# Five of eight row tiles of w_mod[gb] kept in PSUM, transposed, from the modulation stage to the end of the FFN

## The chip, the cores and the metric

The kernel runs on one core of one Trainium2 chip. The metric is device time in microseconds (us), from the start of the program to its end, the median of several executions. PE is TensorE (PEld its weight loads), DVE is VectorE, ACT is ScalarE, POOL is GpSimd and SP is SyncE. "L206" in a profile line is line 206 of the kernel that was profiled; the changed kernel and the experiments have other line numbers for the same helpers (L206 becomes L213, L171 becomes L172).

## The reference, cut to what matters

The program computes one decoder block and its gradients with respect to all its inputs. The block is modulated: six vectors of 1024 come from `silu(c) @ w_mod`, where `w_mod` is 1024 x 6144, six sections of 1024 columns.

```python
mod = (_silu(c) @ w_mod).reshape(c.shape[0], 6, 1, -1)
sa, ca, ga, sb, cb, gb = (mod[:, 0], mod[:, 1], mod[:, 2], mod[:, 3], mod[:, 4], mod[:, 5])
h = _layernorm(x) * (1 + ca) + sa
x = x + ga * _A_ref(h, k_cache, v_cache, wq, wo)      # attention, 4096 keys of 65536
h = _layernorm(x) * (1 + cb) + sb
x = x + gb * _B_ref(h, w_gate, w_up, w_down)          # FFN of 3584
```

The gradient of `c` needs `w_mod @ dmod`: each of the 1024 rows of `w_mod` times the gradient of the six vectors. The part for `gb` (section 5) is `w_mod[:, 5*1024:] @ (grad_out * ffn)`, so it can only be formed after the FFN. The gradients of the caches are zero outside the last 4096 keys, so the kernel must write some 126 MB of zeros.

## The kernel before

`w_mod` is loaded once at the start, in eight row tiles of 128 x 6144 (1.5 MB each). Each tile gives its share of `mod` and is then transposed by PE, section by section, into PSUM; DVE and ACT carry sections 0 to 4 from there to SBUF, where they wait, transposed, for the gradient of `c`. For section 5 the kernel keeps no room in SBUF. It is loaded again at the end (256 KB for each row tile), and DVE forms its product-sum with the gradient.

```python
psum = tc.tile_pool(name="psum", bufs=3, space=PSUM)      # [128, 512] f32, also tm_w
pacc = tc.tile_pool(name="pacc", bufs=2, space=PSUM)      # small accumulators
phold = tc.tile_pool(name="phold", bufs=1, space=PSUM)    # the FFN's sum
ptp = tc.tile_pool(name="ptp", bufs=2, space=PSUM)        # transposes
...
def mod_transpose(j):
    tps = {}
    for sct in (1, 0, 2, 3, 4):
        tp = tps[sct] = new_tp("tp_w") if sct < 2 else new_tm("tm_w")
        for nb in range(KD):
            c0 = sct * D + nb * P
            nc.tensor.transpose(tp[:, nb * P:(nb + 1) * P], wm_t[j][:, c0:c0 + P], ident_bf[:, :])
    ...                                   # evacuations: two on DVE, three on ACT
for j in range(KD):                       # eight row tiles
    for k in range(KM):                   # 48 columns of mod
        mm = nc.tensor.matmul(mod_ps[:, k:k + 1], lhsT=wm_t[j][:, k * P:(k + 1) * P], ...)
    if j < KD - 1:
        mod_transpose(j)
    zero(Z_MOD[j], mm)                    # zero writes, paced by this matmul
    ...
# last stages
def sec_load(j):
    nc.sync.dma_start(out=sec_t[j][:, 3 * D:4 * D], in_=wm_view[:, j, 5 * D:6 * D])
def sec(j, nz):
    w5 = sec_t[j][:, 3 * D:4 * D]
    ttr(w5, w5, dmod_b4[:, 3 * D:4 * D], dcs[:, j:j + 1])      # product-sum on DVE
    outer_dve(sec_t[j], cs_col[:, j:j + 1], dmod_b4)           # gradient of w_mod
    nc.gpsimd.dma_start(out=dwm_view[:, j, 2048:6144], in_=sec_t[j])
    zero(nz)
sec_load(0)
sec_load(1)
for q4 in range(8):                       # dWo: four product-sums, four outer products each
    ...
    nc.gpsimd.dma_start(out=wo_rows(out_5, q4), in_=wo_t[q4])
    zero(Z_DWO[q4])
    ...
# then dS, dq; sec_load(2) to sec_load(7); sec(0), sec(1); dWq with kv gradients and sec(2) to sec(7)
```

POOL issues most writes, among them the zeros: `zero(n)` puts n writes of 1 MB each behind whatever POOL has issued, so that the DMA queues have work while the engines compute. The counts in lists such as `Z_DWO` pace them.

Of the kernel before, what the change touches and what calls it, by code (L numbers as in the profile page):

```python
# [34 lines left out]
SCALE = DH ** -0.5  # L35
KIB = 512


# [23 lines left out]
def kernel(  # L62
# [29 lines left out]
    pool = ctx.enter_context(tc.tile_pool(name="sb", bufs=1))  # L92
    psum = ctx.enter_context(tc.tile_pool(name="psum", bufs=3, space=bass.MemoryType.PSUM))
    pacc = ctx.enter_context(tc.tile_pool(name="pacc", bufs=2, space=bass.MemoryType.PSUM))
    phold = ctx.enter_context(tc.tile_pool(name="phold", bufs=1, space=bass.MemoryType.PSUM))
    ptp = ctx.enter_context(tc.tile_pool(name="ptp", bufs=2, space=bass.MemoryType.PSUM))

# [76 lines left out]


    def new_ps(name="ps"):
        return psum.tile([P, 512], FP32, name=name, tag="mm")

# [3 lines left out]
    def new_tp(name="tp"):  # L182
        return ptp.tile([P, 1024], BF16, name=name, tag="tp")

    def new_tm(name="tm"):
        return psum.tile([P, 1024], BF16, name=name, tag="mm")

# [6 lines left out]
    def addv(out, a, b):  # L194
        return tt(out, a, b, ALU.add)

    def cp(out, a):
        return nc.vector.tensor_copy(out=out, in_=a)  # L198
# [43 lines left out]
    def col_to_row_out(col_f, dram_out_row, name):  # L242
        rp = ptp.tile([8, P], FP32, name="rp_" + name, tag="tp")
        nc.tensor.transpose(rp[:, :], col_f, ident_f[:, :])
        rowb = pool.tile([8, P], BF16, name=name + "_orow", tag=name + "_orow")
        cp(rowb, rp[:, :])
        nc.sync.dma_start(out=dram_out_row.rearrange("o (j p) -> (o j) p", p=P), in_=rowb)
# [73 lines left out]

    tp0 = ptp.tile([P, 24], BF16, name="tp_rows", tag="tp")
    nc.tensor.transpose(tp0[:, :], rows24[:, :], ident_bf[0:24, 0:24])
    vecs = vt([P, 24], "vecs")
    cp(vecs, tp0[:, :])
    x0_col, go_col, c_col = vecs[:, 0:8], vecs[:, 8:16], vecs[:, 16:24]
# [16 lines left out]
    def mod_transpose(j):  # L343
        tps = {}
        for sct in (1, 0, 2, 3, 4):
            tp = tps[sct] = new_tp("tp_w") if sct < 2 else new_tm("tm_w")
            for nb in range(KD):
                c0 = sct * D + nb * P
                nc.tensor.transpose(tp[:, nb * P:(nb + 1) * P], wm_t[j][:, c0:c0 + P], ident_bf[:, :])  # L349
        cols = slice(j * P, (j + 1) * P)  # L350
        v = {k: tp.rearrange("p (n m) -> p n m", n=KD) for k, tp in tps.items()}
        mulv(w01_tmp, v[1], ln1.rearrange("p (n o) -> p n o", o=1).broadcast_to([P, KD, P]))
        addv(w01_T[:, :, cols], w01_tmp, v[0])
        nc.scalar.copy(out=w2_T[:, :, cols], in_=v[2])
        nc.scalar.copy(out=w34_T[:, :, 0, cols], in_=v[3])
        nc.scalar.copy(out=w34_T[:, :, 1, cols], in_=v[4])

    mod_ps = new_acc("mod_ps")
    for j in range(KD):
# [235 lines left out]

    ffn_ps = phold.tile([P, KD], FP32, name="ffn_ps")
    dh2acc = vt([P, NB * KD], "dh2acc")
# [8 lines left out]
    def front(n):  # L606
        ug, wd = ug_slot[n % 3], wd_slot[n % 2]
        r = small[n % 2]
        gu = gu_t[n] = new_acc("gu_ps")
        for col, k in ((2, 0), (0, 1)):  # L610
            for jj in range(2):
                for j in range(KD):
                    nc.tensor.matmul(gu[:, col + jj:col + jj + 1], lhsT=ug[:, k, j, jj::2],  # L613
                                     rhs=h2_bf[:, j:j + 1], start=(j == 0), stop=(j == KD - 1))
        nc.scalar.activation(out=r["sg"], in_=gu[:, 0:2], func=ACT.Sigmoid)  # L615
        nc.scalar.activation(out=r["om"], in_=gu[:, 0:2], func=ACT.Sigmoid, scale=-1.0)
# [50 lines left out]
    ffn = vt([P, KD], "ffn")  # L667
    cp(ffn, ffn_ps[:, :])
    dh2 = vt([P, KD], "dh2")
# [10 lines left out]
    dmod_bf = vt([P, KM], "dmod_bf", BF16)  # L680
    mulv(dmod_bf[:, 40:48], go_col, ffn)
    cp(dmod_bf[:, 24:32], dh2)
# [29 lines left out]
    def sec(j, nz):  # L712
        w5 = sec_t[j][:, 3 * D:4 * D]
        ttr(w5, w5, dmod_b4[:, 3 * D:4 * D], dcs[:, j:j + 1])
        outer_dve(sec_t[j], cs_col[:, j:j + 1], dmod_b4)
        nc.gpsimd.dma_start(out=dwm_view[:, j, 2048:6144], in_=sec_t[j])
        zero(nz)

    sec_load(0)
    sec_load(1)  # L720

# [24 lines left out]
    for q4 in range(8):  # L746
# [10 lines left out]
        if q4 < 2:  # L757
            bcast(dmod_bf[:, 16 + 16 * q4:32 + 16 * q4], 16, dmod_b4[:, 2048 * q4:2048 * (q4 + 1)], "A")
        elif q4 < 6:
            rebuild_P(q4 - 2)  # L760
        elif q4 == 6:
            build_e()
# [24 lines left out]
    for ch in range(8):  # L787
        ps = new_ps("dp_ps")
        for g in range(G):
# [4 lines left out]
                                       in1=P_bf[:, ch * 512:(ch + 1) * 512], op0=ALU.subtract, op1=ALU.mult)  # L794
    sec_load(2)
    sec_load(3)
    dsT = transpose_rows(dS, "dsT", "AAAA")
    DO_hd = make_hd(do_col2, "DO_hd")
    sec(0, Z_SEC[0])
    dq_ps, mm = av_like(k_nat, dsT, "dq")  # L800
    for k in range(4, 8):
        sec_load(k)
# [109 lines left out]
```

## Time and profile before

| | before |
|---|---|
| median of 4 executions | 624.12 us (623.96 to 624.36) |
| span of the profiled execution | 622.2 us |
| moved by DMA | 256.42 MB, mean 412 GB/s |
| busiest engine | DVE, 326.3 us (52%) |

From the groups by shape (line, engine, operation, output <- inputs, shapes, count | busy us, mean ns | idle time before and what ended it): the product of a transposed PSUM tile with a vector, and the product-sums of section 5.

```profile
L189 DVE TENSOR_TENSOR arena<-tp_w,ln_ln 128x1024 f32<-128x1024 bf16 x8 | 9.8, 1224 | 16.2 <-PE tp_w L349 16.2
L206 DVE CUSTOM_DVE_ANT_0 arena<-arena 128x1024 bf16<-128x1024 bf16 x8 | 9.8, 1219 | 29.9 <-DMA arena<-in_w_mod_dram 29.9
```

The reader is to see the durations, 1.22 us each, and that all the idle time before the product-sums, 29.9 us, is one wait for the reloads.

From the timeline of PE in the modulation stage (start, duration, count): the 48 `mod` matmuls of two consecutive row tiles.

```profile
25.67 1.35 PE L361 MATMUL mod_ps<-cs_bf,arena 128*128 128x1 bf16 x48 [0.57 <-DMA arena<-in_w_mod_dram]
29.25 1.35 PE L361 MATMUL mod_ps<-cs_bf,arena 128*128 128x1 bf16 x48
```

One row tile takes 3.6 us here. What PE waits for is data (0.57 us before the first of the two); no wait for a bank shows.

### The profile page before, as it was taken

The numbers are of one execution on the slowest core, as the hardware profiler recorded it, in microseconds if no ns is written. First come the engines' busy times: TensorE is split into PE (matmuls) and PEld (weight loads), VectorE is DVE, ScalarE is ACT, GpSimd is POOL, SyncE is SP. The second block draws the span as 40 slices with busy tenths as digits, with TensorE's granted clock in tenths as the row PEclk, the third lists the DMA queues.
The fourth block names the chain that finished last, engine by engine and source line by source line (L and its number), as shares of the span: only waits on it lengthen the run. The fifth ranks groups of instructions, "written<-read, shape, count | busy, mean of one in ns | idle before, by whom it ended". The sixth has DMA issues, their size and how long they took to land.

```text
span 622.2 us, 8426 instructions
## 1 busy us (share of the span) xinstructions
PE 186.5 (30%) x3324; PEld 163.6 (26%) x3324; DVE 326.3 (52%) x728; ACT 212.5 (34%) x333; POOL 148.2 (24%) x232
## 2 busy tenths in 40 slices
PE   3977266623022111111011111133039100455100
PEld 3967155623012111111011111122017100344100
DVE  3442037302969385544556554469997306994400
ACT  2652147200026143322133333239847101455300
POOL 2001021113222433223343322342211111222420
PEclk9976578755555555555555555555557555555555
DMA  9999999999999999999999999999999999999997
GB/s 351 422 421 421 421 418 420 423 425 423 423 403 408 408 410 410 411 411 408 411 411 409 411 412 409 413 419 414 427 426 421 423 424 419 428 426 425 423 424 273
DMA packets 42647, 256.42 MB, mean 412 GB/s; under 512 B 5149, under 2 KB 5149, under 8 KB 18080
## 3 DMA queue, kind: packets, MB, share of 16 engines
q0 software_dynamic: 31568, 192.95, 80.6%
q1 hardware_dynamic: 10992, 62.93, 29.9%
q8 instruction: 26, 0.43, 0.3%
q14 instruction: 13, 0.11, 0.0%
q10 hardware_dynamic: 48, 0.01, 0.0%
HBM read 70.26 MB, written 185.60 MB: 411 GB/s over the span
## 4 chain that ended last, share of the span: by engine, by line
DMA 59%; DVE 12%; issue 11%; PE 8%; POOL 4%; ACT 3%; ACTq 0%; POOLq 0%; SPq 0%; DVEq 0%
DMA out_dram<-arena 28%; DMA out_dram<-zeros 11%; DVE arena L206 7%; DMA arena<-in_w_mod_dram 6%; DMA arena<-in_B_w_gate_dram 5%; DMA arena<-in_A_k_cache_dram 4%; DMA arena<-in_B_w_down_dram 3%; PE tp_kv L440 2%; ACT arena L443 1%; PE tm_w L349 1%; DVE arena L202 1%; POOL out_dram L657 1%; POOL arena L540 1%; POOL out_dram L171 1%; PE tp_w L349 1%
## 5 line engine op out<-in xcount | busy, mean ns | idle before, releaser
L171 POOL DMA_DIRECT2D out_dram<-zeros x114 | 63.0, 556 | 179.8 <-DMA out_dram<-zeros 55.5
L237 ACT ACTIVATE arena<-dug_b,h 128x512 bf16<-128x512 bf16 x112 | 71.4, 713 | 13.3 <-DVE dh2acc L206 13.3
L206 DVE CUSTOM_DVE_ANT_0 arena<-arena,dug_b 128x512 bf16<-128x512 bf16 x112 | 69.6, 686 | 0.1
L206 DVE CUSTOM_DVE_ANT_0 arena<-arena 128x1024 bf16<-128x1024 bf16 (+1 forms) x16 | 45.1, 2819 | 32.3 <-DMA arena<-in_w_mod_dram 29.9
L613 PE MATMUL gu_ps<-h_bf,arena 128*128 128x1 bf16 x448 | 16.2, 166 | 144.8 <-issue 92.1
L613 PEld LDWEIGHTS <-arena 128*128 128x128 bf16 x448 | 14.2, 105 | 146.9 <-issue 92.6
L206 DVE CUSTOM_DVE_ANT_0 junk<-arena,b1k 128x1024 fp8e4<-128x1024 bf16 x28 | 34.3, 1224 | 29.3 <-DMA arena<-in_B_w_down_dram 28.8
L823 PEld LDWEIGHTS <-arena 8*128 8x128 bf16 x256 | 24.9, 127 | 72.9 <-issue 69.5
L615 ACT ACTIVATE sg<-gu_ps 128x2 f32<-128x2 f32 x14 | 2.4, 168 | 111.0 <-PE gu_ps L613 111.0
L206 DVE CUSTOM_DVE_ANT_0 arena<-arena,b1k 128x1024 bf16<-128x1024 bf16 x32 | 37.2, 1220 | 0.0
L540 POOL DMA_DIRECT2D arena<-in_B_w_up_dram x14 | 12.8, 918 | 88.8 <-DMA out_dram<-arena 48.3
L827 ACT CAST arena<-ps_kv 128x512 bf16<-128x512 f32 x32 | 16.1, 692 | 44.2 <-DMA out_dram<-arena 44.2
L237 ACT ACTIVATE arena<-b1k,o_sh 128x1024 bf16<-128x1024 bf16 x24 | 27.2, 1151 | 11.0 <-DVE do_sh L206 11.0
L189 DVE TENSOR_TENSOR dug<-dhh,sg 128x2 f32<-128x2 f32 x14 | 2.3, 161 | 53.5 <-ACT sg L615 52.9
L440 PE MATMUL tp_kv<-ident_bf,arena 128*128 128x128 bf16 x256 | 22.4, 255 | 21.5 <-DMA arena<-in_A_k_cache_dram 13.8
L823 PE MATMUL ps_kv<-DO_hd,arena 8*128 8x128 bf16 x128 | 15.3, 279 | 45.0 <-ACT arena L827 44.2
L198 DVE COPY arena<-tp_kv 128x1024 bf16<-128x1024 bf16 x19 | 13.1, 691 | 29.2 <-PE tp_kv L440 29.2
L637 PE MATMUL bc_ps<-ident_bf,dug_bf 128*128 128x128 bf16 x56 | 14.5, 475 | 44.9 <-DVE hh L189 44.9
L440 PEld LDWEIGHTS <-arena 128*128 128x128 bf16 x256 | 19.6, 116 | 24.3 <-DMA arena<-in_A_k_cache_dram 14.7
L349 PEld LDWEIGHTS <-arena 128*128 128x128 bf16 x320 | 24.9, 121 | 0.0
L443 ACT COPY arena<-tp_kv 128x1024 bf16<-128x1024 bf16 x13 | 13.1, 1010 | 32.5 <-PE tp_kv L440 32.5
L829 ACT ACTIVATE arena<-ps_kv 128x512 bf16<-128x512 f32 x32 | 16.1, 625 | 21.6 <-DMA out_dram<-arena 21.6
(228 smaller groups left out, 503.8 us busy)
## 6 DMA issues: line engine op xcount, KB each, us to landing
out_dram<-zeros POOLq DMA_DIRECT2D x114, 1024.0 KB, 16.3
out_dram<-arena POOLq DMA_DIRECT2D x32, 1024.0 KB, 17.7
out_dram<-arena POOLq DMA_DIRECT2D x36, 512.0 KB, 13.3
arena<-in_A_wq_dram SPq DMA_DIRECT2D x16, 1024.0 KB, 15.8
arena<-in_w_mod_dram SPq DMA_DIRECT2D x8, 1536.0 KB, 20.3
arena<-in_A_wo_dram SPq DMA_DIRECT2D x8, 1024.0 KB, 39.7
arena<-in_B_w_down_dram SPq DMA_DIRECT2D x14, 512.0 KB, 11.5
arena<-in_B_w_up_dram POOLq DMA_DIRECT2D x14, 512.0 KB, 11.7
```

The lines of the kernel that those rows point to most:

```text
L171: ins = nc.gpsimd.dma_start(out=region.bitcast(FP32), in_=zeros[:, :])
L206: return nc.vector.tensor_tensor_reduce(out=out, in0=w, in1=b, scale=1.0, scalar=0.0, op0=ALU.mult, op1=ALU.add, accum_out=acc)
L237: return nc.scalar.activation(out=out, in_=b, func=ACT.Copy, scale=col)
L349: nc.tensor.transpose(tp[:, nb * P:(nb + 1) * P], wm_t[j][:, c0:c0 + P], ident_bf[:, :])
L440: nc.tensor.transpose(tp[:, t8 * P:(t8 + 1) * P], src[:, g, t_ * DH:(t_ + 1) * DH], ident_bf[:, :])
L443: last = nc.scalar.copy(out=o, in_=tp[:, :])
L540: nc.gpsimd.dma_start(out=ug_slot[n % 3][:, k, :, :], in_=view[:, :, n * FB:(n + 1) * FB])
L613: nc.tensor.matmul(gu[:, col + jj:col + jj + 1], lhsT=ug[:, k, j, jj::2], rhs=h2_bf[:, j:j + 1], start=(j == 0), stop=(j == KD - 1))
L637: nc.tensor.matmul(ps4[:, k // 2, :, k % 2], lhsT=r["dug_bf"][:, k:k + 1].broadcast_to([P, P]), rhs=ident_bf[:, :], start=(k == 0), stop=( ...
L823: nc.tensor.matmul(ps[:, t4 * DH:(t4 + 1) * DH], lhsT=rows[32 * g:32 * g + HG, t_ * P:(t_ + 1) * P], rhs=hd[32 * g:32 * g + HG, :], start= ...
L827: nc.scalar.copy(out=o, in_=ps[:, :])
L829: nc.scalar.activation(out=o, in_=ps[:, :], func=ACT.Copy, scale=float(scale))
```

## The change

The intent is to save reloads without room in SBUF. PSUM has eight banks; a transposed row tile of section 5 (128 x 1024 bf16) fills one. Five tiles stay parked there from the modulation stage to the end of the FFN. Everything else shares three banks: two that rotate, for transposes and for [128, 512] results alike, and one accumulator. At the end of the FFN the parked tile is multiplied with the gradient vector (which lies along the partitions, since the tile is transposed), summed over its eight blocks, and summed over the partitions by a matmul with ones. After that the five banks join the rotation. Three reloads remain. The diff, cut to its core:

```diff
+PARK = 5
-    psum = ... name="psum", bufs=3
-    pacc = ... name="pacc", bufs=2
-    phold = ... name="phold", bufs=1
-    ptp = ... name="ptp", bufs=2
+    psum = ... name="psum", bufs=7 - PARK
+    pacc = ... name="pacc", bufs=1
+    ppark = ... name="ppark", bufs=PARK
     ...
     def mod_transpose(j):
-        tps = {}
         for sct in (1, 0, 2, 3, 4):
-            tp = tps[sct] = new_tp("tp_w") if sct < 2 else new_tm("tm_w")
+            tp = new_tp("tp_w")
             ...                                # transposes, then at once the evacuation
+        if j < PARK:
+            park[j] = ppark.tile([P, D], BF16, name="park", tag="pk")
+            for nb in range(KD):
+                c0 = 5 * D + nb * P
+                nc.tensor.transpose(park[j][:, nb * P:(nb + 1) * P], wm_t[j][:, c0:c0 + P], ident_bf[:, :])
     ...
-    ffn_ps = phold.tile([P, KD], FP32, name="ffn_ps")
+    ffn_ps = new_acc("ffn_ps")[:, 0:KD]
-        gu = gu_t[n] = new_acc("gu_ps")
+        gu = gu_t[n] = new_ps("gu_ps")
     ...
-        ttr(w5, w5, dmod_b4[:, 3 * D:4 * D], dcs[:, j:j + 1])
+        if j >= PARK:
+            ttr(w5, w5, dmod_b4[:, 3 * D:4 * D], dcs[:, j:j + 1])
-    sec_load(0)
-    sec_load(1)
+    def park_products():
+        prod = dS.bitcast(FP32)
+        pm = prod[:, 0:D].rearrange("p (n m) -> p n m", n=KD)
+        col = dgb.rearrange("p (n o) -> p n o", o=1).broadcast_to([P, KD, P])
+        for j in range(PARK):
+            mulv(pm, park[j].rearrange("p (n m) -> p n m", n=KD), col)
+            nc.vector.reduce_sum(out=prod[:, D + j * P:D + (j + 1) * P], in_=pm.rearrange("p n m -> p m n"), axis=AX.X)
+        ps = new_acc("gb_ps")
+        for j in range(PARK):
+            nc.tensor.matmul(ps[:, j:j + 1], lhsT=prod[:, D + j * P:D + (j + 1) * P], rhs=ones_f[:, 0:1], ...)
+        cp(dcs[:, 0:PARK], ps[:, 0:PARK])
     ...
         elif q4 < 6:
+            if q4 == 2:
+                park_products()
+                rot.append((ppark, "pk"))
             rebuild_P(q4 - 2)
     ...
-    sec_load(2)
-    sec_load(3)
+    for k in range(PARK, 4):
+        sec_load(k)
     ...
-    for k in range(4, 8):
+    for k in range(max(PARK, 4), 8):
         sec_load(k)
```

More of the change, by code (lines that the diff above doesn't have):

```diff
@@ L92 @@
     pool = ctx.enter_context(tc.tile_pool(name="sb", bufs=1))
-    psum = ctx.enter_context(tc.tile_pool(name="psum", bufs=3, space=bass.MemoryType.PSUM))
-    pacc = ctx.enter_context(tc.tile_pool(name="pacc", bufs=2, space=bass.MemoryType.PSUM))
-    phold = ctx.enter_context(tc.tile_pool(name="phold", bufs=1, space=bass.MemoryType.PSUM))
-    ptp = ctx.enter_context(tc.tile_pool(name="ptp", bufs=2, space=bass.MemoryType.PSUM))
+    psum = ctx.enter_context(tc.tile_pool(name="psum", bufs=7 - PARK, space=bass.MemoryType.PSUM))
+    pacc = ctx.enter_context(tc.tile_pool(name="pacc", bufs=1, space=bass.MemoryType.PSUM))
+    ppark = ctx.enter_context(tc.tile_pool(name="ppark", bufs=PARK, space=bass.MemoryType.PSUM))
     arena = pool.tile([P, 192 * KIB], BF16, name="arena")
@@ L173, in zero, with next_pool @@
                 dep(first or ins, after)
+    rot = [(psum, "mm")]
+    nrot = [0]
+    def next_pool():
+        nrot[0] += 1
+        return rot[nrot[0] % len(rot)]
     def new_ps(name="ps"):
-        return psum.tile([P, 512], FP32, name=name, tag="mm")
+        p, tag = next_pool()
+        return p.tile([P, 512], FP32, name=name, tag=tag)
     def new_acc(name="acc"):
@@ L182, in new_tp @@
     def new_tp(name="tp"):
-        return ptp.tile([P, 1024], BF16, name=name, tag="tp")
-    def new_tm(name="tm"):
-        return psum.tile([P, 1024], BF16, name=name, tag="mm")
+        p, tag = next_pool()
+        return p.tile([P, 1024], BF16, name=name, tag=tag)
     def tt(out, a, b, op):
@@ L242, in col_to_row_out @@
     def col_to_row_out(col_f, dram_out_row, name):
-        rp = ptp.tile([8, P], FP32, name="rp_" + name, tag="tp")
-        nc.tensor.transpose(rp[:, :], col_f, ident_f[:, :])
+        rp = new_ps("rp_" + name)[0:8, 0:P]
+        nc.tensor.transpose(rp, col_f, ident_f[:, :])
         rowb = pool.tile([8, P], BF16, name=name + "_orow", tag=name + "_orow")
-        cp(rowb, rp[:, :])
+        cp(rowb, rp)
         nc.sync.dma_start(out=dram_out_row.rearrange("o (j p) -> (o j) p", p=P), in_=rowb)
@@ L320 @@
     nc.gpsimd.dma_start(out=rest[NS:8, 0:nlen * 128], in_=zeros[0:8 - NS, 0:nlen * 128])
-    tp0 = ptp.tile([P, 24], BF16, name="tp_rows", tag="tp")
-    nc.tensor.transpose(tp0[:, :], rows24[:, :], ident_bf[0:24, 0:24])
+    tp0 = new_tp("tp_rows")[:, 0:24]
+    nc.tensor.transpose(tp0, rows24[:, :], ident_bf[0:24, 0:24])
     vecs = vt([P, 24], "vecs")
-    cp(vecs, tp0[:, :])
+    cp(vecs, tp0)
     x0_col, go_col, c_col = vecs[:, 0:8], vecs[:, 8:16], vecs[:, 16:24]
@@ L343, in mod_transpose @@
     def mod_transpose(j):
-        tps = {}
+        cols = slice(j * P, (j + 1) * P)
         for sct in (1, 0, 2, 3, 4):
-            tp = tps[sct] = new_tp("tp_w") if sct < 2 else new_tm("tm_w")
+            tp = new_tp("tp_w")
             for nb in range(KD):
@@ L349, in mod_transpose @@
                 nc.tensor.transpose(tp[:, nb * P:(nb + 1) * P], wm_t[j][:, c0:c0 + P], ident_bf[:, :])
-        cols = slice(j * P, (j + 1) * P)
-        v = {k: tp.rearrange("p (n m) -> p n m", n=KD) for k, tp in tps.items()}
-        mulv(w01_tmp, v[1], ln1.rearrange("p (n o) -> p n o", o=1).broadcast_to([P, KD, P]))
-        addv(w01_T[:, :, cols], w01_tmp, v[0])
-        nc.scalar.copy(out=w2_T[:, :, cols], in_=v[2])
-        nc.scalar.copy(out=w34_T[:, :, 0, cols], in_=v[3])
-        nc.scalar.copy(out=w34_T[:, :, 1, cols], in_=v[4])
+            v = tp.rearrange("p (n m) -> p n m", n=KD)
+            if sct == 1:
+                mulv(w01_tmp, v, ln1.rearrange("p (n o) -> p n o", o=1).broadcast_to([P, KD, P]))
+            elif sct == 0:
+                addv(w01_T[:, :, cols], w01_tmp, v)
+            elif sct == 2:
+                nc.scalar.copy(out=w2_T[:, :, cols], in_=v)
+            else:
+                nc.scalar.copy(out=w34_T[:, :, sct - 3, cols], in_=v)
+        if j < PARK:
[3 more added lines that the diff above has]
+                nc.tensor.transpose(park[j][:, nb * P:(nb + 1) * P], wm_t[j][:, c0:c0 + P], ident_bf[:, :])
+    park = {}
     mod_ps = new_acc("mod_ps")
@@ L667 @@
     ffn = vt([P, KD], "ffn")
-    cp(ffn, ffn_ps[:, :])
+    cp(ffn, ffn_ps)
     dh2 = vt([P, KD], "dh2")
@@ L680 @@
     dmod_bf = vt([P, KM], "dmod_bf", BF16)
-    mulv(dmod_bf[:, 40:48], go_col, ffn)
+    dgb = vt([P, KD], "dgb")
+    mulv(dgb, go_col, ffn)
+    cp(dmod_bf[:, 40:48], dgb)
     cp(dmod_bf[:, 24:32], dh2)
@@ L717, in sec @@
         zero(nz)
-    sec_load(0)
-    sec_load(1)
+    def park_products():
[7 more added lines that the diff above has]
+        for j in range(PARK):
+            nc.tensor.matmul(ps[:, j:j + 1], lhsT=prod[:, D + j * P:D + (j + 1) * P], rhs=ones_f[:, 0:1],
+                             start=True, stop=True)
+        cp(dcs[:, 0:PARK], ps[:, 0:PARK])
     def rebuild_P(tb):
```

## The prediction

> **What bounds the kernel now.** I read the page's slices first. The first line below is the busy share of the 16 DMA engines in 40 equal slices of the span (9 means 90% or more), the second what they moved in each, the third the total.
>
> ```profile
> DMA  9999999999999999999999999999999999999997
> GB/s 351 422 421 421 421 418 420 423 425 423 423 403 408 408 410 410 411 411 408 411 411 409 411 412 409 413 419 414 427 426 421 423 424 419 428 426 425 423 424 273
> DMA packets 42647, 256.42 MB, mean 412 GB/s; under 512 B 5149, under 2 KB 5149, under 8 KB 18080
> ```
>
> The reader is to see that no slice but the first and the last falls off: outside the FFN (403 to 419) the queues move 418 to 428 GB/s whatever the engines do. 256.42 MB at 412 GB/s is 622 us, the whole span. So the kernel is bound by the bytes it moves, and a change is worth the bytes that it removes, unless it lets the queues run dry.
>
> Second, the windows view (columns: length, busy time and count of PE, weight loads, DVE, ACT, POOL; granted clock, DMA share, GB/s), for the stretches that the change touches late in the kernel:
>
> ```profile
> 430.00:440.00 10.00, 2.83 (x104) 2.46 (x96) 9.93 (x17) 8.62 (x9) 2.79 (x5) 0.50 1.14 428
> 440.00:450.00 10.00, 0.91 (x36) 0.64 (x24) 9.93 (x19) 8.68 (x8) 2.13 (x4) 0.50 1.12 426
> 450.00:460.00 10.00, 0.00 (x0) 0.10 (x1) 9.87 (x22) 7.35 (x7) 1.60 (x3) 0.50 1.18 424
> 490.00:518.00 28.00, 0.00 (x0) 0.00 (x0) 0.00 (x0) 0.00 (x0) 3.22 (x6) 0.50 1.08 423
> 518.00:567.00 49.00, 19.35 (x156) 15.68 (x156) 48.56 (x39) 20.04 (x40) 11.09 (x17) 0.50 1.05 425
> ```
>
> From 430 to 460 us DVE is full, from 490 to 518 us all compute engines do nothing, and the DMA rate is the same in both. The listing of waits says what the 28 us are, and what holds POOL, which issues most of the writes:
>
> ```profile
> POOL out_dram L171 <- DMA out_dram<-zeros: 55.5, 35, 3.2
> DVE arena L206 <- DMA arena<-in_w_mod_dram: 29.9, 1, 29.9
> ```
>
> POOL waits for earlier zero writes to land before it may issue more: the write queue is full. DVE waits once, 29.9 us, for reloaded w_mod rows, the very transfers that the change partly removes. Those 29.9 us look like the prize; they are not, because the DMA works through them.
>
> Third, how deep the queue is. A 1024 KB zero write takes 16.3 us from issue to landing in the median (the page's DMA issues), but 1.05 MB at 424 GB/s is only 2.5 us, so some 14 us of other work stands ahead of it. Summing bytes issued minus bytes of packets ended over the trace gives the same: 5 to 8 MB outstanding (12 to 19 us) from 405 to 520 us, 6.8 to 9 MB from 25 to 60 us, and minima of 2.5 MB (6 us) near 140 us and 2.0 MB (5 us) near 575 us.
>
> **What the Trainium skill says.** "DMA: Bandwidth & Descriptors", section "Where 436 GB/s comes from", puts the ceiling of the 16 ports at 435 GB/s; the trace agrees, with 418 to 428 held for most of the span: there is no faster rate to win, only fewer bytes. "VectorE: DVE Perf Modes", sections "The perf-mode tier table" and "Why PSUM operands drop a tier", says that a product of two tensors with one in PSUM, and any reduction, runs at one element a cycle; the trace agrees for the product: 128x1024 from a transposed PSUM tile takes 1224 ns. "PSUM — Partial Sum Buffer", "Specifications (TRN2)": 8 banks of 2 KiB a partition; a transposed 128x1024 bf16 tile fills one, so five parked tiles leave three. "TensorE: Matmul & The Clock Gate", Part 1, says that idleness halves the PE clock; here eight transposes take about 0.93 us before 21 us and 0.52 us at 22 to 33 us, so a PE that waits more may also run slower.
>
> **The change part by part.**
>
> (a) Removed: five of the eight w_mod reloads at the end, 256.0 KB each: 5 x 262,144 B = 1.31 MB. At the 424 GB/s of that stretch: 3.1 us of DMA time, on the path, since the DMA is the path. Also five product-sums 128x1024 of 1.22 us (the x8 group: 1219 ns), 6.1 us of DVE beside it.
>
> (b) Added on DVE, in the dWo stage after the third of eight blocks: five products from PSUM at 1.22 us (same shape and types as the 128x1024 f32<-bf16 rows of the modulation stage) and five strided f32 reductions of 1024. No row has this reduction; my estimate from one element a cycle is 1.2 us, and from the 128x112 strided row (0.35 us, 1.9 ns an element above a small one's 0.15) 2.0 us. Sum 12 to 16 us, plus about 1 us for five small f32 matmuls and a copy: 13 to 17 us of DVE in a stage where DVE is full. Is it on the path? POOL issues the dWo blocks late because its queue is full. In the timeline (start, duration, line; in brackets its idle time):
>
> ```profile
> 447.89 0.53 POOL L755 DMA_DIRECT2D out_dram<-arena  x1 [2.25 <-ACT arena L237]
> 450.32 0.53 POOL L755 DMA_DIRECT2D out_dram<-arena  x1 [1.90 <-DVE do_sh L206]
> 452.75 0.53 POOL L755 DMA_DIRECT2D out_dram<-arena  x1 [1.90 <-ACT arena L237]
> ```
>
> These are blocks 2, 3 and 4, which DVE finished at about 434, 439 and 444 us: POOL lags DVE by 9 to 14 us. Delayed by 15 us, block 3 is ready at 454 and block 4 at 459, so they go out 4 and 6 us late, against 17 us outstanding at 450 us (7.3 MB). The queue thins, but doesn't empty. The chain after it (dS, dq, first dWq) starts about 15 us later; then the 29.9 us wait is gone for rows 2 to 4, which need no reload, so DVE makes up what it lost. I expect DVE's work through the last dWq to end before the 567 us of before. The ends of the last stage are set by the two kv-gradient buffers coming free, as before.
>
> (c) Moved to fewer banks: the modulation stage rotates two banks where it had five, so each of the five section transposes waits for an evacuation (DVE 1.22 us, ACT 1.02 us). Per row tile, worked out by hand: tile pair 1.0, product 1.2, sum 1.2, then copies of 1.0 chained with the transposes, then eight parked transposes 0.5 and the 48 columns of mod 1.3: about 5.9 us with the fast clock, 7.5 with the slow, against 3.6 and 5.6 in the trace. PE falls 6 to 8 us behind, of which later tiles' waits for data take back little: q starts at about 60 us, not 52.5. Parked transposes: 40 x 65 to 117 ns = 2.6 to 4.7 us of PE, in that sum. Loads of w_mod 5 to 7 and of K are issued later by the same, but 6.8 to 9 MB are outstanding then (16 to 21 us). By my sum at least 4 MB stay ahead. So hidden.
>
> (d) FFN, scores and kv gradients: gate/up results and broadcasts now share two banks, but each is read before its bank is next wanted; the FFN total takes the one accumulator bank, which nothing else wants meanwhile; after the parked products the five banks join the rotation. I charge nothing.
>
> Sum: 624.0 - 3.1 = 620.9 us.
>
> **The rivals.** 1, the path is DVE's: the chain that ended last runs through DVE product-sums from 418 to 459 us and through the w_mod reload at 502 us. If the chain were the bound, +15 us of DVE and -30 us of wait would give about 610 us, or 637 if the wait is not recovered. Against it: the DMA moves 423 to 428 GB/s through both stretches. 2, the queue runs dry: either at 60 to 68 us, if PE stays at the slow clock in the modulation stage (K loads 12 or more us late), or near 450 to 490 us, if the reductions cost more than 2 us each. Each dry microsecond adds one; I could believe 2 to 5 us, giving 621 to 626. 3, a transfer that is hidden anyway: if the 1.31 MB only filled gaps, the time would stay 624; but no gap shows in the slices where they move. 4, fewer holes at the end: 2.0 MB outstanding at 575 us goes with 410 GB/s, so an earlier DVE could win a few tenths.
>
> **Range and chances.** The byte term is firm (2.9 to 3.3 us). Rival 2 is the main spread, upward; rival 4 is small, downward. Predicted 620.9 us, 8 in 10 between 619.6 and 624.0. Faster by over 2% needs 611.5 us, four times the bytes removed: 0.01. Slower by over 2% needs 636.5 us, 15 us of empty queue: 0.02. Within 2%: 0.97.
>
> **What would show it.** Moved bytes 255.1 MB instead of 256.4 at the same mean rate (411 to 413 GB/s). The 29.9 us wait gone or below 10 us, without the time following it. Products at 1.2 us, reductions 1.2 to 2 us; DVE 13 to 17 us busier around 434 to 450 us with 415 to 428 GB/s kept. q's matmuls starting at 58 to 64 us, still 418 or more GB/s before and after. The prediction is wrong if a slice in the middle falls below 400 GB/s, or if the span falls by much more than bytes over rate.

## The result, and the profile after

| | before | after |
|---|---|---|
| median | 624.12 us (4 executions, 623.96 to 624.36) | 620.90 us (4 executions, 620.81 to 621.34) |
| ratio | 1 | 0.9949, 95% interval 0.9932 to 0.9967 |
| span of the profiled execution | 622.2 us | 619.0 us |
| moved by DMA | 256.42 MB | 255.11 MB |
| DVE busy | 326.3 us | 335.4 us |

A ratio is the mean time of one kernel's executions over that of the other's of the same rounds, so it is not quite the ratio of the medians quoted. The result lies within 2%: 3.2 us, 0.5%.

The page of the changed kernel, as the prediction showed it for the one before: busy share of the DMA engines in 40 slices, what they moved, the total.

```profile
DMA  9999999999999999999999999999999999999997
GB/s 350 424 424 420 397 420 423 425 420 425 425 405 402 410 412 409 412 405 412 411 412 409 411 409 411 412 415 421 426 425 425 422 422 423 425 427 425 427 421 287
DMA packets 41927, 255.11 MB, mean 412 GB/s; under 512 B 5069, under 2 KB 5069, under 8 KB 17360
```

The reader is to see the same mean rate, 412 GB/s, 1.31 MB fewer, and one new flaw: the fifth slice (62 to 77 us) fell to 397 GB/s.

The windows view for that stretch, kernel before and then kernel after (columns as in the prediction: length, busy time and count of PE, weight loads, DVE, ACT, POOL; granted clock, DMA share, GB/s):

```profile
62.00:77.00 15.00, 4.11 (x56) 3.24 (x56) 0.98 (x3) 1.95 (x2) 1.64 (x4) 0.50 1.13 421
```

```profile
62.00:77.00 15.00, 10.65 (x290) 10.40 (x290) 1.66 (x5) 2.94 (x3) 3.16 (x6) 0.50 1.05 398
430.00:450.00 20.00, 2.85 (x12) 2.40 (x10) 19.21 (x17) 3.85 (x5) 4.79 (x9) 0.50 1.13 427
490.00:518.00 28.00, 10.65 (x92) 9.12 (x91) 23.71 (x13) 10.76 (x22) 6.31 (x10) 0.50 1.08 422
518.00:567.00 49.00, 19.72 (x160) 16.33 (x160) 32.92 (x29) 20.10 (x40) 10.79 (x18) 0.50 1.05 426
```

From 490 to 518 us, where all compute engines had idled, DVE is now busy for 23.7 of 28 us, and the DMA moves 422 GB/s instead of 423. What the engines do there does not matter to the time.

What the added work costs on DVE, from the groups by shape:

```profile
L744 DVE TENSOR_REDUCE arena<-arena 128x128 f32<-128x1024 f32 x5 | 9.4, 1871 | 0.2
L196 DVE TENSOR_TENSOR arena<-park,dgb 128x1024 f32<-128x1024 bf16 x5 | 6.1, 1223 | 0.1
```

Products of 1.22 us and reductions of 1.87 us: with starts 3.2 us apart, 16.5 us from 433.8 to 450.3 us, the copy included. The timeline of POOL shows what that delays (dWo blocks 2, 3 and 4, now L784):

```profile
447.35 0.53 POOL L784 DMA_DIRECT2D out_dram<-arena  x1 [2.23 <-DMA out_dram<-zeros]
456.05 0.53 POOL L784 DMA_DIRECT2D out_dram<-arena  x1 [8.17 <-DVE arena L209]
461.14 0.53 POOL L784 DMA_DIRECT2D out_dram<-arena  x1 [4.56 <-ACT arena L759]
```

Block 3 goes out at 456.0 instead of 450.3 us and block 4 at 461.1 instead of 452.8 us, and POOL now waits for DVE there, 8.2 us. The queue (the bytes issued and not yet moved) held 7.0 MB at 450 us and at least 4.1 MB from there to 500 us, so the rate did not move.

The chain that ended last, by line, is a trap worth seeing:

```profile
DMA out_dram<-arena 29%; DMA out_dram<-zeros 21%; DMA arena<-in_B_w_gate_dram 5%; DVE arena L213 4%; DVE arena L196 4%; DMA arena<-in_B_w_down_dram 3%; PE tp_w L356 3%; PE mod_ps L377 2%; DVE arena L744 2%; POOL out_dram L673 1%; POOL arena L556 1%; DMA rows<-in_c_dram 1%; PE q_ps L416 1%; POOL out_dram L172 1%; DVE arena L209 1%
```

It runs through the reductions (L744) and the products (part of L196) that were just added. Yet the kernel got faster, and nothing of them shows in the time: it fell by what the bytes are worth.

In the modulation stage, two consecutive row tiles on PE:

```profile
25.07 1.34 PE L377 MATMUL mod_ps<-cs_bf,arena 128*128 128x1 bf16 x48
31.87 1.34 PE L377 MATMUL mod_ps<-cs_bf,arena 128*128 128x1 bf16 x48
```

6.8 us a row tile instead of 3.6. The PE clock, by its records, changes between half and full every 3.4 us here. The q matmuls began at 64.9 us (before: 52.6 us). K and V loads wait for this stage's tiles to come free, and zero writes wait for the q matmuls, so the queue ran down to 0.8 MB at 64 us. Bytes moved up to a given time, summed from the packets' ends, put a number on it:

```
time us   before MB   after MB   difference, in us of 420 GB/s
   60       23.95       24.03      +0.2
   90       36.53       36.19      -0.8
  410      168.48      168.15      -0.8
  490      202.09      201.93      -0.4
  610      252.97      252.80      -0.4
```

So this execution lost 0.8 us in the modulation stage and kept the loss through the FFN. It had 1.31 MB less to move (3.1 us), regained 0.4 us between 410 and 490 us, and the last packets and the end of the program gained the rest: the span is 3.1 us shorter.

### The profile page after: what moved, and what is told of

It reads as the page before. It is cut to its first block, busy times and chain, and to the rows that moved or that the text cites. A ratio compares the mean times of both kernels' runs of the same rounds, so it can differ in the third digit from the quotient of the medians.

```text
span 619.0 us, 8520 instructions
## 1 busy us (share of the span) xinstructions
PE 196.1 (32%) x3374; PEld 172.6 (28%) x3374; DVE 335.4 (54%) x730; ACT 213.8 (35%) x333; POOL 148.8 (24%) x232
## 2 busy tenths in 40 slices
DMA packets 41927, 255.11 MB, mean 412 GB/s; under 512 B 5069, under 2 KB 5069, under 8 KB 17360
## 3 DMA queue, kind: packets, MB, share of 16 engines
HBM read 68.95 MB, written 185.60 MB: 411 GB/s over the span
## 4 chain that ended last, share of the span: by engine, by line
DMA 59%; DVE 13%; issue 11%; PE 9%; POOL 4%; ACT 1%; ACTq 0%; POOLq 0%; DVEq 0%; SPq 0%
DMA out_dram<-arena 29%; DMA out_dram<-zeros 21%; DMA arena<-in_B_w_gate_dram 5%; DVE arena L213 4%; DVE arena L196 4%; DMA arena<-in_B_w_down_dram 3%; PE tp_w L356 3%; PE mod_ps L377 2%; DVE arena L744 2%; POOL out_dram L673 1%; POOL arena L556 1%; DMA rows<-in_c_dram 1%; PE q_ps L416 1%; POOL out_dram L172 1%; DVE arena L209 1%
## 5 line engine op out<-in xcount | busy, mean ns | idle before, releaser
L172 POOL DMA_DIRECT2D out_dram<-zeros x114 | 63.0, 554 | 189.6 <-DMA out_dram<-zeros 61.5
L629 PEld LDWEIGHTS <-arena 128*128 128x128 bf16 x448 | 14.3, 105 | 142.8 <-DMA arena<-in_B_w_up_dram 95.8
L213 DVE CUSTOM_DVE_ANT_0 arena<-arena 128x4096 bf16<-128x4096 bf16 (+1 forms) x11 | 39.0, 3546 | 4.8 <-ACT arena L302 4.8
L356 PE MATMUL tp_w<-ident_bf,arena 128*128 128x128 bf16 x320 | 33.7, 285 | 8.5 <-DVE arena L196 8.5
L356 PEld LDWEIGHTS <-arena 128*128 128x128 bf16 x320 | 29.3, 132 | 10.9 <-issue 10.9
L196 DVE TENSOR_TENSOR dug<-dhh,sg 128x2 f32<-128x2 f32 x14 | 2.2, 160 | 51.9 <-ACT sg L631 51.5
L196 DVE TENSOR_TENSOR arena<-tp_w,ln_ln 128x1024 f32<-128x1024 bf16 x8 | 9.8, 1223 | 26.8 <-PE tp_w L356 26.8
L861 ACT ACTIVATE arena<-ps_kv 128x512 bf16<-128x512 f32 x32 | 16.1, 627 | 20.8 <-DMA out_dram<-arena 20.8
L855 PE MATMUL ps_kv<-Q_hd,arena 8*128 8x128 bf16 x128 | 15.8, 302 | 21.1 <-ACT arena L861 21.1
L556 POOL DMA_DIRECT2D arena<-in_B_w_gate_dram x14 | 12.7, 910 | 39.5 <-issue 20.7
```

The lines of the kernel that those rows point to most:

```text
L172: ins = nc.gpsimd.dma_start(out=region.bitcast(FP32), in_=zeros[:, :])
L196: return nc.vector.tensor_tensor(out=out, in0=a, in1=b, op=op)
L213: return nc.vector.tensor_tensor_reduce(out=out, in0=w, in1=b, scale=1.0, scalar=0.0, op0=ALU.mult, op1=ALU.add, accum_out=acc)
L556: nc.gpsimd.dma_start(out=ug_slot[n % 3][:, k, :, :], in_=view[:, :, n * FB:(n + 1) * FB])
L629: nc.tensor.matmul(gu[:, col + jj:col + jj + 1], lhsT=ug[:, k, j, jj::2], rhs=h2_bf[:, j:j + 1], start=(j == 0), stop=(j == KD - 1))
L855: nc.tensor.matmul(ps[:, t4 * DH:(t4 + 1) * DH], lhsT=rows[32 * g:32 * g + HG, t_ * P:(t_ + 1) * P], rhs=hd[32 * g:32 * g + HG, :], start= ...
```

## The experiments

The theory: the time is the bytes over a rate of some 420 GB/s, plus whatever time the queues run dry; waits and engine time count only if they make them dry. The main rival: the gain comes from the wait of 29.9 us that vanished, or from what VectorE does (the chain runs through it). A second rival: the two-bank rotation takes something back.

"Queue" below is the bytes of all DMAs issued up to a moment less the bytes of the packets ended by then. The experiments of one call ran on the same chip, against executions of the kernel before on it (medians 624.00 to 624.09 us).

**Control.** The experiments avoid one instruction form of the kernel, the product-sum with an fp8 output: its element-wise output goes to a scratch tile that nobody reads. All of them store it as uint8.

```diff
-    junk = vt([P, D], "junk", FP8)
+    junk = vt([P, D], "junk", mybir.dt.uint8)
```

> Control: the changed kernel with one scratch tile of the FFN (the element-wise output of the product-sums, which nobody reads) stored as uint8 instead of fp8; every later experiment carries this edit. Both theories: 620.9 us, within 0.3 us of the changed kernel, product-sums of 128x1024 still 1.22 us. If it is off by more, the others are compared with this control.

Measured: 620.85 us (5 executions, 620.71 to 621.41), ratio 0.9950, interval 0.9937 to 0.9962. The edit is neutral, and the control stands for the changed kernel.

**The bytes put back, without the wait.** The five reloads return. They are issued when they were before, two at 418 us and three from 503 us (before: 417 and 502 us). Three go into the room of a row tile that is filled later, two into their own, long before it is written; no engine reads them.

```diff
+    sec_load(0)
+    sec_load(1)
     ...
+    for k in range(2, PARK):
+        nc.sync.dma_start(out=sec_t[5][:, (k - 2) * D:(k - 1) * D], in_=wm_view[:, k, 5 * D:6 * D])
     for k in range(max(PARK, 4), 8):
         sec_load(k)
```

> The changed kernel with the five removed 256 KB reloads put back at their old places, into room that nobody reads from, so that no engine waits for them: bytes as before, wait gone, parked products kept. Bytes theory: 1.31 MB at 0.42 MB/us come back, 624.0 us (623.7 to 624.5), same as the kernel before. Wait theory (the gain is the 29.9 us wait of VectorE, or a freer VectorE): stays near 620.9 us.

Measured: 624.19 us (624.05 to 624.69), ratio 1.0002, interval 0.9990 to 1.0015. From its page and its listing of waits:

```profile
DMA packets 42647, 256.42 MB, mean 412 GB/s; under 512 B 5149, under 2 KB 5149, under 8 KB 18080
```

```profile
DVE arena L213 <- DMA arena<-in_w_mod_dram: 1.7, 1, 1.7
```

The bytes are those of the kernel before, DVE waits 1.7 us for reloads instead of 29.9 us, and the time is that of the kernel before. The wait was worth nothing that the interval of ±0.8 us shows; the bytes are the gain.

**The wait kept, without the bytes.** Of the six rows that the last loop handles, the three that are still reloaded come first.

```diff
-            sec(1 + i, Z_SEC[1 + i])
+            sec([5, 6, 7, 2, 3, 4][i - 1], Z_SEC[1 + i])
```

> The changed kernel with the order of the w_mod row tiles of the last stage turned so that the three that are still reloaded come first: bytes gone, but VectorE waits again some 10 to 15 us for a reload near 505 to 518 us. Bytes theory: 620.9 us (up to 0.5 us more). Wait theory: the gain is lost in part or whole, 622.5 to 624 us or more.

Measured: 621.02 us (620.71 to 621.59), ratio 0.9951, interval 0.9937 to 0.9964.

```profile
DMA packets 41927, 255.11 MB, mean 412 GB/s; under 512 B 5069, under 2 KB 5069, under 8 KB 17360
```

```profile
DVE arena L213 <- DMA arena<-in_w_mod_dram: 11.8, 1, 11.8
```

11.8 of the 29.9 us of DVE wait come back and the gain stays (in proportion, 1.2 us would have gone; the interval is ±0.8 us). With the run before it, this takes the main rival from both sides.

**How the gain goes with the number of tiles.** Three parked tiles (`PARK = 3`), and, with a wrong gradient of `c` on purpose, the changed kernel without its last three reloads and their product-sums.

```diff
-PARK = 5
+PARK = 3
```

> Three parked tiles instead of five (four rotating banks, five reloads): bytes theory with 0.62 us per tile gives 624.1 - 1.9 = 622.2 us, and with four banks there is no dip in the modulation stage, so 621.6 to 622.4 us. A theory in which the gain does not go with the number of tiles (a wait that vanishes): 620.9 us, or 624.1 us.

Measured: 622.31 us (622.10 to 622.98), ratio 0.9974, interval 0.9962 to 0.9986, 255.63 MB.

```diff
-        if j >= PARK:
+        if False:
             ttr(w5, w5, dmod_b4[:, 3 * D:4 * D], dcs[:, j:j + 1])
-    for k in range(max(PARK, 4), 8):
-        sec_load(k)
+    nc.vector.memset(dcs[:, PARK:8], 0.0)
```

> Wrong on purpose (the gradient of c lacks a term): the changed kernel without its last three reloads and their product-sums. Bytes theory: 0.79 MB less than the changed kernel, 1.9 us at 0.42 MB/us, 619.0 us (618.7 to 619.3). A theory in which the gain ends when no wait is left: 620.9 us.

Measured: 619.78 us (5 executions: 620.06, 619.87, 619.78, 618.80, 618.71), ratio 0.9923, interval 0.9910 to 0.9936, 254.32 MB; the gradient of `c` is wrong, as said, all else right. By the ratios and the mean of 624.1 us, three, five and eight reloads fewer are worth 1.6, 3.1 and 4.8 us: 0.5 to 0.6 us each, against 0.62 us from 262,144 B at 420 GB/s. The last run missed its range of 618.7 to 619.3 us: three of five executions lie 0.5 to 0.8 us above it, two at its lower end. Its profiled execution is the longest, and there the queue ran down to 0.4 MB at 65 us and lost 1.5 us by 90 us, twice what the changed kernel lost. The next two runs are on that.

**Two rotating banks alone.** The pools of the changed kernel, nothing parked, all reloads as before.

```diff
-PARK = 5
+PARK = 0
+BANKS = 5
-    psum = ... bufs=7 - PARK
-    ppark = ... bufs=PARK
+    psum = ... bufs=7 - BANKS
+    ppark = ... bufs=BANKS
     ...                                   # sec_load(0) to (3) as before; no park_products()
```

> Two rotating banks alone: the pools of the changed kernel, but nothing is parked, all eight reloads and their product-sums stay as before, no products from PSUM. In the changed trace the modulation stage drained the queue to 1.5 MB near 65 us and moved 0.8 us worth of bytes less by 90 us; the parked transposes are some 0.7 us per tile of that stage. Bytes theory: 624.1 us plus 0.3 to 0.8 us for this dip, so 624.4 to 625.0. A theory in which fewer banks are free: 624.1 us. A theory in which two banks also cost in the FFN: over 626 us.

Measured: 624.54 us (624.26 to 624.83), ratio 1.0006, interval 0.9994 to 1.0019. The expected few tenths fit, but the interval includes zero, and the profiled execution shows no dip (420 GB/s in the slice from 62 to 77 us, q from 62.3 us, 0.1 us behind at 90 us). What is shown is that two banks cost nothing like 2 us in the FFN.

**Zero writes moved to where the queue thins.**

```diff
-Z_MOD = [1, 0, 0, 0, 0, 0, 0, 0]
-Z_Q = [0, 1, 0, 0, 0, 0, 4, 1]
+Z_MOD = [1, 0, 0, 0, 2, 0, 0, 0]
+Z_Q = [0, 1, 0, 0, 0, 0, 2, 1]
```

> The changed kernel with two of the four zero writes that wait for the q matmuls (near 72 us) moved up behind the fifth row tile's mod matmuls (near 40 us), where the write queue is empty: the same bytes, two 1 MB writes earlier. Theory that the two-bank modulation stage costs 0.8 us because the queue thins to 1.5 MB near 65 us: the dip goes and the time falls by 0.4 to 0.8 us, to 620.0 to 620.5 us. Theory that these 0.8 us are noise or are made up later anyway: 620.9 us. Theory that the writes delay the wq and K loads and with them the attention: over 621.3 us.

Measured: 620.77 us (620.34 to 621.18), ratio 0.9948, interval 0.9936 to 0.9961. The mechanism worked: the queue held 4.6 MB or more throughout the stage, the DMA moved 422 GB/s from 62 to 77 us, and the bytes at 90 us were 0.2 us ahead of the kernel before. The time is that of the control within 0.1 us, with intervals of ±0.8 us. So a gain is not shown. The profiled executions say that the dip varies from one to the next. "Full clock" is how long PE had its full clock between 10 us and the start of q, by the clock records; "least queue" is from steps of 0.1 us:

```
execution            q begins   full clock   least queue   GB/s, 62 to 77 us   behind the kernel before at 90 us
no reloads            66.0 us     17.1 us       0.4 MB           378                1.5 us
changed kernel        64.9 us     17.1 us       0.8 MB           398                0.8 us
control               63.8 us     21.9 us       1.1 MB           404                0.6 us
products three times  63.7 us     20.5 us       1.3 MB           413                0.1 us
bytes back            63.5 us     21.9 us       1.3 MB           409                0.5 us
products twice        61.7 us     27.2 us       2.0 MB           421                0.0 us
wait kept             61.3 us     30.7 us       2.5 MB           420                0.4 us
products twice, fed   61.1 us     30.7 us       2.4 MB           419                0.1 us
zero writes moved     60.8 us     30.7 us       4.6 MB           422                0.2 us ahead
```

All but the last have the same program up to there. On the whole q begins later, and the queue is thinner, the shorter the clock was full. One execution shows both speeds; four starts of the 48 `mod` matmuls in the run with the wait kept, whose clock records begin with full clock from 27.5 to 58.2 us:

```profile
19.10 1.46 PE L377 MATMUL mod_ps<-cs_bf,arena 128*128 128x1 bf16 x48
26.59 1.44 PE L377 MATMUL mod_ps<-cs_bf,arena 128*128 128x1 bf16 x48
32.48 1.34 PE L377 MATMUL mod_ps<-cs_bf,arena 128*128 128x1 bf16 x48
38.26 1.34 PE L377 MATMUL mod_ps<-cs_bf,arena 128*128 128x1 bf16 x48
```

A row tile with a parked section takes 7.5 us before that record and 5.8 us at full clock; sixteen transposes in a row take 1.87 us (at 24.1 us) and 1.05 us (at 31.1 us). The changed kernel's 6.8 us lie between, with a clock that alternates. So the dip goes with the clock that an execution happens to get in this stage. No run set the clock, and what decides it was not isolated.

**The products twice and three times.** This loads the step that the prediction leaned on: that 16 us of DVE are hidden by the depth of the queue.

```diff
                 park_products()
+                park_products()
```

> The changed kernel with the parked products computed twice (same result): 15.9 us more of VectorE at 450 us, the same bytes. The queue holds 7.0 MB (17 us) at 447 us and the next dWo block then comes at 472 us rather than 456 us. Theory that the queue's depth is what hides VectorE: it now runs dry for some microseconds near 465 to 500 us, 624 to 632 us. Theory that the idle time of VectorE (29.9 us in the kernel before) hides it: 620.9 to 621.5 us. Theory that VectorE is the path: 636 us or more.

Measured: 626.77 us (625.92 to 628.74), ratio 1.0046, interval 1.0033 to 1.0059. Three times:

> The parked products three times: 31.8 us more of VectorE than the changed kernel. Queue theory: what exceeds the queue's depth shows in full, so 14 to 16 us more than with two times: 638 to 648 us. Idle-time theory: about 29.9 us can be hidden, so under 624 us.

Measured: 645.97 us (645.62 to 647.11), ratio 1.0353, interval 1.0340 to 1.0367. The first 16.5 us of products cost nothing that shows (the bytes alone account for the 3.1 us gained), the second 5.9 us, the third 19.2 us. The windows from 465 to 482 us, first of the changed kernel, then of the one with the products twice, with the issue of dWo block 3 in the latter:

```profile
465.00:482.00 17.00, 4.25 (x44) 1.98 (x44) 15.65 (x36) 8.46 (x9) 2.65 (x5) 0.50 1.05 425
```

```profile
465.00:482.00 17.00, 4.55 (x146) 4.26 (x146) 16.25 (x27) 12.54 (x12) 1.59 (x3) 0.60 0.68 256
```

```profile
473.11 0.53 POOL L784 DMA_DIRECT2D out_dram<-arena  x1 [25.48 <-DVE arena L209]
```

POOL waits 25.5 us for DVE. The queue holds 6.7 MB at 450 us, 1.3 MB at 465 us and nothing at 470 us, and the rate falls to 256 GB/s: 6.7 us worth of bytes short by 490 us. The page of the run with three (GB/s of 40 slices) has two slices at a quarter to a third of the rate, and a third, later, at 365:

```profile
GB/s 357 424 420 422 411 420 424 423 420 427 418 397 413 408 407 409 411 412 412 410 410 411 409 412 411 417 421 425 419 105 137 425 365 423 425 427 426 428 420 290
```

A slice is 16.1 us, so 365 instead of some 425 GB/s is worth 2.3 us (an estimate); that fits the 2.7 us by which the third set cost more than its 16.5 us.

**The products twice, with the queue fed.** If it is the queue, zero writes in the right place must take the loss away, although VectorE's work stays.

```diff
                 park_products()
+                park_products()
-Z_DWO = [3, 4, 0, 0, 1, 2, 0, 0]
-Z_SEC = [1, 1, 3, 0, 1, 1, 4, 1]
+Z_DWO = [3, 4, 3, 0, 1, 2, 0, 0]
+Z_SEC = [1, 1, 0, 0, 1, 1, 4, 1]
```

> The parked products twice, as in the run that took 626.8 us and whose queue stood empty near 465 to 482 us, but with three zero writes moved from the last stage (after the third w_mod tile) to just after dWo block 2, ahead of the gap of 25 us in POOL's issues: same bytes, same 16 us more of VectorE. Queue theory: the three MB cover the 2.8 MB that were missing, so the time returns to 620.9 to 621.6 us. Theory that VectorE's extra 16 us are themselves on the path: stays near 626.8 us.

Measured: 621.15 us (621.06 to 621.17), ratio 0.9950, interval 0.9936 to 0.9964. The same window:

```profile
465.00:482.00 17.00, 4.53 (x146) 4.27 (x146) 16.25 (x27) 12.53 (x12) 2.32 (x4) 0.60 1.11 411
```

DVE does the same 16.25 us of work in it, the DMA moves 411 GB/s instead of 256, and 5.6 us are back. The path is the queue and not VectorE.

**Six parked tiles, one rotating bank.**

```diff
-PARK = 5
+PARK = 6
```

> Six parked tiles, so that one bank rotates. If only bytes counted: 620.3 us. But in the modulation stage each section transpose now waits for the evacuation before it: about 10 us a row tile by the durations of the changed trace (5 transposes and evacuations in a row 5 x 1.7, parked 0.7, mod 1.3) instead of 6.8, q some 25 us later, against a queue that was already down to 1.5 to 2.7 MB (4 to 6 us) there: it runs dry for about 20 us, 635 to 650 us.

Measured: 687.61 us (687.38 to 687.78), ratio 1.1015, interval 1.0999 to 1.1031: much worse than expected. The page (GB/s), and two of the transposes of eight on PE:

```profile
GB/s 355 426 263 328 63 123 344 423 394 76 124 417 412 422 395 409 409 407 412 410 410 411 410 411 412 412 411 413 416 427 425 426 423 421 427 425 424 426 421 301
```

```profile
62.31 1.01 PE L356 MATMUL tp_w<-ident_bf,arena 128*128 128x128 bf16 x8 [1.31 <-DVE arena L196]
66.75 1.01 PE L356 MATMUL tp_w<-ident_bf,arena 128*128 128x128 bf16 x8 [1.10 <-ACT arena L363]
```

Each transpose of a section waits for the evacuation before it, 1.31 us for DVE or 1.10 us for ACT, so a row tile takes 11.9 us and not the 10 estimated, and q starts at 104 us. Part of the difference is the clock: eight transposes take 1.01 us, as at half clock above, not 0.61 us. The second reason is that the attention stage rotates the same bank: the transposes of K and V alternate with their copies, and two more slices, near 154 to 188 us, are at 76 and 124 GB/s. By the bytes moved, the run is 40 us behind the kernel before at 130 us and 67 us at 200 us. The expectation had only the modulation stage in it.

**Zero writes moved, and another order of the sections.**

```diff
-        for sct in (1, 0, 2, 3, 4):
+        for sct in (1, 2, 0, 3, 4):
     ...                                   # and Z_MOD, Z_Q as in the run with zero writes moved
```

> The changed kernel with the two zero writes moved up (as in the filler run, 620.8 us) and the section order 1, 2, 0, 3, 4 in place of 1, 0, 2, 3, 4, so that VectorE and ScalarE empty the two banks in turn: about 6 us a row tile instead of 6.8, q 4 to 6 us earlier. Same bytes, a queue that stays over 4 MB: 620.3 to 620.9 us, at most 0.5 us better than the changed kernel. If shortening this stage were worth what it saves: 615 to 617 us.

Measured: 620.81 us (620.63 to 621.15), ratio 0.9945, interval 0.9933 to 0.9958. The order did not do what it was for: a row tile still takes 6.9 us (the third transpose waits 0.87 us for DVE), and q began at 67.7 us, later than in any run of the table. Yet no dip shows: 423 GB/s from 62 to 77 us, with never less than 1.8 MB in the queue, two zero writes having been moved up. No version is shown to beat the changed kernel.

## Why the prediction was right or wrong

- **The bound and the byte term: right, and the reason is shown.** 3.1 us were predicted for the bytes; the time fell by 3.2 us, to the predicted 620.9 us. Bytes back without the wait gave 624.19 us, the wait back without the bytes 621.02 us, and three, five and eight reloads gave 1.6, 3.1 and 4.8 us.
- **DVE's added work (b): right in size and in effect.** 13 to 17 us were predicted, 16.5 us measured (they displaced other work from 434 to 450 us, where DVE was full before and after, and did not make it busier there); the reductions took 1.87 us, near the upper of the two estimates, the one taken from the strided row. That they are hidden by the queue's depth is shown from both sides: doubled, they cost 5.9 us, and 0.3 us once the queue was fed. Blocks 3 and 4 went out 5.7 and 8.4 us late, not 4 and 6.
- **The 29.9 us wait: right.** It is gone, and worth nothing.
- **The end of DVE's dWq work**, predicted before 567 us, is right: by the timelines it ended at 550.6 us, before the change at 566.9 us.
- **Step (c): the row tile was right, the clock and the queue were not.** "At least 4 MB stay ahead" is wrong: 0.8 MB in the profiled execution, 0.4 to 2.5 MB in others of the same stage. The period worked out by hand, 5.9 us with the fast clock and 7.5 us with the slow, is what the traces show (5.8 and 7.5 us). But q at 60 us took the clock as fast for the whole stage; it changed between the two, and q began at 64.9 us, 12.3 us late, which is rival 2 in the modulation stage ("12 or more us late"). And the queue is 5.8 MB at its lowest there in the kernel before (at 52.3 us), not 6.8 MB. An estimate from these: 5.8 MB less 0.42 MB for each us that q is late gives 0.7 MB (measured 0.8 MB), and 2.2 MB for the run with the wait kept (8.7 us late; measured 2.5 MB). The prediction's own 6.8 MB and 8 us give 3.4 MB and not 4. The dip lost 0.8 us in that execution, less than the 2 to 5 us that the rival was given. The total was right all the same because about as much came back: 0.4 us between 410 and 490 us, and the rest at the end of the program. Where these came from was not isolated, so part of the exactness is luck.
- **Step (d), no charge for the FFN: right within what can be resolved.** Two banks alone cost 0.4 us, with an interval that includes zero.
- **What was to be seen:** 255.11 MB at 412 GB/s, as said. The prediction's own sign of being wrong, a middle slice below 400 GB/s, came about, at 397, and q began outside its 58 to 64 us; both are step (c), and neither touches the byte term.
- **Slips in its figures.** Its queue depths are samples some us apart; in steps of 0.1 us the range is 5.8 to 9.7 MB from 25 to 60 us and 4.4 to 9.9 MB from 405 to 520 us, with minima of 1.7 MB at 142 us and 2.1 MB at 567 us. The rate from 570 to 580 us was 419 GB/s, not 410. Its 637 us for an unrecovered wait should be 639 by its own 15 us. None of these carries the result.

## What to carry to other kernels

When nearly every slice of the profile shows the DMA at one rate, count bytes first: here the change was worth the bytes that it removed over that rate, and neither the idle engine nor the chain that ended last said anything of the gain. Work added to an engine was free here up to the depth of the queue in front of the gap that it made, and cost about in full beyond that; so compare the gap with the bytes outstanding there, and move other writes ahead of it before giving the work up. A buffer that sits unused for most of a program can save a reload, but the buffers left over must still keep apart every producer from the evacuation of its predecessor: two banks did here, one cost 67 us. And when a hidden stage depends on PE, work it out with both clocks, and compare the slower with the queue at its lowest.

## What the Trainium skill lacked or had wrong

- "DMA: Bandwidth & Descriptors", section "Where 436 GB/s comes from", says that for transfers between HBM and SBUF the HBM side, about 358 GB/s, binds. That sentence has no condition, and it does not hold for the one core that runs here: outside the FFN it moved 418 to 428 GB/s for over 300 us (kernel before), with 185.60 MB written to HBM and 70.26 MB read. The 425 GB/s that the page measured for one core alone is what the run shows, and the 435 GB/s of the ports is the nearer ceiling.
- "VectorE: DVE Perf Modes", section "The perf-mode tier table", gives a reduction one element a cycle. The 128x1024 fp32 reduction that reads with a step of 512 B took 1871 ns, 1.8 ns an element; a contiguous maximum over 128x512 bf16 in the kernel before took 677 ns, 1.3 ns an element with its fixed part. The penalty for leaving a 16-byte line stands on another page, "SBUF — State Buffer", section "Door 1: The DMA port swizzle", without a size; this run fits it, though no run here varied the step alone.
- No page tells how far POOL's writes run ahead and when POOL is held back. Here POOL's share of the queue stayed at or below 7.6 MB, and POOL waited 55.5 us before and 61.5 us after the change for earlier zero writes to land.
- "TensorE: Matmul & The Clock Gate" warns that clock records are unreliable. One form of it that it lacks: until the first record a trace reads as full clock. In the run with six parked tiles the first record is at 557 us and the windows before it read 1.00, while eight transposes took 1.01 us, against 1.05 us for sixteen in the kernel before at 22.7 us.
